# Spreading transfers over the steps of retention attention, and an earlier first product of the experts

## The chip, the cores and the metric

The kernel runs on one core of a Trainium2 chip. The metric is the time of one execution on the device in microseconds, as the median of several runs. The engines are named as in the profile: PE is TensorE (PEld its weight loads), DVE VectorE, ACT ScalarE, POOL GpSimd, and SP is SyncE, which here only issues transfers.

## The reference

The reference is retention attention followed by a mixture of experts.

```python
# q, k, v: 4 batches, 8 heads, 768 tokens, 64 wide
gamma = 1.0 - 2.0 ** (-5.0 - np.arange(H))
for t in range(S):
    state = gamma * state + k[t] (outer) v[t]          # per batch and head
    y[t] = q[t] @ state / sqrt(D)
x = y as 3072 tokens of 512
noisy = x @ w_gate + log1p(exp(x @ w_noise)) * noise    # 8 experts
top2 of noisy per token, weights by softmax over the two
out[token] += weight * (relu(x[token] @ w1[e]) @ w2[e])  # w1: 512x1024, w2: 1024x512
```

## The kernel before, in words

The 3072 tokens are 24 chunks of 128. One call of `step(j)` works on several chunks at once: PE multiplies q and k of chunk j+1 (`qk`, 8 matmuls into `pA`; the trace counts each fp32 matmul as two), turns the result of chunk j-1 (`x_turn`, into `pT`), adds the state's part of y for chunk j (`y_state`), adds the chunk's own part (`y_mm`, from the masked products `am` and the scaled values `vp`) and updates the state (`pU`, which ACT copies to U). DVE masks `pA` into `am`, works out the scale of a token row, and copies y out of PSUM as `yt`. ACT takes the sum of squares, the logits, `x` (L459) and its fp16 half. POOL makes `vp` (`v_scale`) and the low fp16 half of x (L465). SP issues the loads of chunk j+4 (`load`, 512 KB for q and k, 512 KB for v and k), and stores x into a buffer in memory (`x_store`). `AHEAD` is 4, so five tiles of each input are there. The order of the work on each engine is the order in which the program issues it; there is no planner. Work of other kinds is put at the end of a step by small tables: `at` and `P` with the number of the step (`todo`, `mid`), `at0` (`first_todo`, at the very end), and `middle` between `y_state` and `y_mm`.

Tokens' routing is worked out in three groups during and after the steps (`route_x` and what follows it). The experts' matmuls run in fp16 with each number split into a high and a low half. For the first expert this preparation lies in the steps: `w_load` brings a quarter of w1 (512 KB) into `wst`, `w_sum` takes squares on ACT, `w_scale` adds them on PE into the PSUM bank pR, DVE makes a power of two of it, `w_hi` rounds to fp16 on ACT, and `w_lo_half` makes half of a low part on DVE. The first expert's first 384 tokens are fetched from the buffer by three `gather` calls (an indirect DMA issued by POOL) and turned by three DMA transposes issued by SP (`x_t`), which write the tile `xe`. The first product of the experts (`first(0, ...)`, 12 matmuls of 384 columns, L918, L919 and L923) follows the last step; x_turn(23) stands in its middle. After it PE goes through all other products.

`HALVES` and `WHOLE` choose the form of `x_turn`: a chunk in `WHOLE` uses 4 matmuls of 128x144 (and a memset on DVE), the others 16 of 64x80.

## Time and profile before

| | |
|---|---|
| median of 3 runs | 643.45 us (642.65 to 644.96) |
| the profiled execution | 642.6 us, span 640.8 us, mean granted clock of TensorE 0.997 of full speed |
| PE busy | 627.5 us (98%) |
| ACT, DVE, POOL busy | 302.7, 290.4, 203.1 us |
| steps 0 to 23 | from the start to 110.40 us, where the second product begins |
| DMA | 113.03 MB, mean 176 GB/s |

The profiled execution took 1.8 us more than its span; the median of the three runs is 0.85 us above the profiled execution. Times in rows count from the span's start. A name in square brackets at a row's end is what the engine waited for; "issue" means that the profile shows nothing that it waited for.

### The profile page before, as it was taken

To read this page: it belongs to the slowest core of one execution; us is meant where nothing else is said; L and a number is where in the kernel's file an instruction comes from. 1 tells how busy PE (TensorE), PEld (TensorE's weight loads), DVE (VectorE), ACT (ScalarE), POOL (GpSimd) and SP (SyncE) were. 2 spreads that over 40 slices of the span, in tenths; PEclk is the share of its full clock that TensorE was granted. 3 is DMA by queue.
4 is the path that set the end of the run, shared out by engine and by line. 5 is a ranking of instruction groups with operands and counts; after the bars stand their busy time and mean duration, and the time that the engine had idled before them with its cause. 6 is when DMAs were issued, how large, how long until landed. Compare 5 with 4: busy or idle time off the path is not lost.

```text
span 640.8 us, 12702 instructions
## 1 busy us (share of the span) xinstructions
PE 627.5 (98%) x5151; PEld 380.8 (59%) x5151; DVE 290.4 (45%) x747; ACT 302.7 (47%) x582; POOL 203.1 (32%) x169
## 2 busy tenths in 40 slices
PE   9999989999999999999999999999999999999995
PEld 6888877559488545554455445544554465455574
DVE  4667887997453222653162236222622262215020
ACT  5688557516553443454344445434543454344121
POOL 2555575041530143114420432043304420430214
PEclk9999999999999999999999999999999999999998
DMA  8999995988868167727673667457744774572313
GB/s 304 407 408 405 351 370 135 368 198 294 177 133 262 25 110 137 266 44 133 115 222 108 104 129 209 133 94 127 209 142 87 135 202 141 97 125 44 42 18 43
DMA packets 87656, 113.03 MB, mean 176 GB/s; under 512 B 59910, under 2 KB 61068, under 8 KB 84012
## 3 DMA queue, kind: packets, MB, share of 16 engines
q1 hardware_dynamic: 75808, 85.56, 42.8%
q0 software_dynamic: 11776, 26.63, 22.5%
q8 instruction: 41, 0.67, 0.4%
q14 instruction: 19, 0.16, 0.1%
q10 hardware_dynamic: 12, 0.01, 0.0%
HBM read 72.66 MB, written 26.42 MB: 155 GB/s over the span
## 4 chain that ended last, share of the span: by engine, by line
PE 92%; DMA 3%; DVE 2%; ACT 1%; issue 1%; POOL 1%; SPq 0%; POOLq 0%; ACTq 0%
PE pH L918 13%; PE pH L919 13%; PE pH L921 13%; PE pO L967 12%; PE pO L969 12%; PE pO L968 12%; PE pA L368 3%; PE pY L392 3%; PE pT L1023 2%; PE pT L426 2%; DMA wst<-w 2%; PE pO L1011 2%; PE pY L385 2%; PE pT L416 1%; PE pU L402 1%; DMA in_vk<-vk 1%
## 5 line engine op out<-in xcount | busy, mean ns | idle before, releaser
L958 POOL DMA_INDIRECT out<-ot,idx x51 | 82.2, 1612 | 317.8 <-ACT ot L953 194.9
L918 PE MATMUL pH<-xe,w1h 128*128 128x384 f16 (+5 forms) x576 | 180.9, 314 | 0.1
L919 PE MATMUL pH<-xe,w1h 128*128 128x384 f16 (+5 forms) x576 | 180.8, 314 | 0.0
L921 PE MATMUL pH<-xe,w1l 128*128 128x384 f16 (+5 forms) x572 | 179.6, 314 | 0.0
L930 DVE SCALAR_TENSOR_TENSOR hl<-pH,hh 128x384 f16<-128x384 f32 (+5 forms) x144 | 75.6, 526 | 140.3 <-ACT hh L927 139.7
L969 PE MATMUL pO<-w2h,hl 128*128 128x512 f16 x344 | 130.4, 379 | 0.0
L968 PE MATMUL pO<-w2l,hh 128*128 128x512 f16 x344 | 130.4, 379 | 0.0
L967 PE MATMUL pO<-w2h,hh 128*128 128x512 f16 x344 | 130.4, 379 | 0.0
L927 ACT ACTIVATE hh<-pH 128x384 f16<-128x384 f32 (+5 forms) x144 | 67.1, 466 | 122.9 <-PE pH L921 112.1
L953 ACT ACTIVATE ot<-pO,gse 128x512 f32<-128x512 f32 x45 | 30.9, 687 | 155.1 <-PE pO L969 143.0
L240 DVE SCALAR_TENSOR_TENSOR w1l<-wst,wsc,w1h 128x1024 f16<-128x1024 f32 x28 | 35.9, 1284 | 95.4 <-ACT w1h L235 95.4
L918 PEld LDWEIGHTS <-w1h 128*128 128x128 f16 x576 | 56.3, 98 | 33.1 <-issue 2.7
L919 PEld LDWEIGHTS <-w1h 128*128 128x128 f16 x576 | 56.3, 98 | 30.1 <-issue 0.3
L921 PEld LDWEIGHTS <-w1l 128*128 128x128 f16 x572 | 55.9, 98 | 30.7
L771 POOL DMA_INDIRECT xg<-xbuf,idx x54 | 56.2, 1041 | 34.5 <-DVE idx L684 18.1
L212 ACT ACTIVATE junk<-wst 128x1024 bf16<-128x1024 f32 x64 | 67.0, 1047 | 0.3 <-DMA wst<-w 0.3
L969 PEld LDWEIGHTS <-hl 128*128 128x128 f16 x344 | 33.6, 98 | 40.6
L967 PEld LDWEIGHTS <-hh 128*128 128x128 f16 x344 | 33.6, 98 | 40.6 <-issue 0.4
L968 PEld LDWEIGHTS <-hh 128*128 128x128 f16 x344 | 33.6, 98 | 39.6
L465 POOL TENSOR_TENSOR x<-x,x 128x512 f16<-128x512 f32 x23 | 28.0, 1218 | 38.3 <-ACT x L464 17.8
L235 ACT ACTIVATE w2h<-wst,wsc 128x1024 f16<-128x1024 f32 x32 | 36.5, 1140 | 0.7 <-DVE wsc L190 0.7
L235 ACT ACTIVATE w1h<-wst,wsc 128x1024 f16<-128x1024 f32 x32 | 36.2, 1137 | 0.3 <-DVE wsc L190 0.3
(193 smaller groups left out, 661.8 us busy)
## 6 DMA issues: line engine op xcount, KB each, us to landing
wst<-w SPq DMA_DIRECT2D x28, 1024.0 KB, 7.6
in_qk<-qk SPq DMA_DIRECT2D x24, 512.0 KB, 8.2
in_vk<-vk SPq DMA_DIRECT2D x23, 512.0 KB, 8.3
xbuf<-x SPq DMA_DIRECT2D x24, 256.0 KB, 6.6
out<-zero SPq DMA_DIRECT2D x6, 1024.0 KB, 8.2
wst<-w SPq DMA_DIRECT2D x8, 512.0 KB, 7.3
xg<-xbuf,idx POOLq DMA_INDIRECT x54, 4.8
xe<-xg SPq DMA_TRANSPOSE x54, 4.7
```

Source lines behind the costliest of these rows:

```text
L212: nc.scalar.activation(junk, st[:, i * 1024:(i + 1) * 1024], AF.Square, accum_out=ss[:, i:i + 1])
L235: nc.scalar.activation(hi, st[:, i * 1024:(i + 1) * 1024], AF.Copy, scale=sc[:, 0:1])
L771: nc.gpsimd.indirect_dma_start(out=x[:n], out_offset=None, in_=xbuf[:128 + B0 * S] if e == 0 and t < 3 else xbuf, in_offset=bass.IndirectO ...
L918: nc.tensor.matmul(p[:, :n], whi, xh, start=(k == 0), stop=False)
L919: nc.tensor.matmul(p[:, :n], whi, xl, start=False, stop=False)
L921: nc.tensor.matmul(p[:, :n], wlo, xh, start=False, stop=(k == KT - 1))
L927: nc.scalar.activation(hh[:, f, n0:n1], p, AF.Relu)
L930: nc.vector.scalar_tensor_tensor(hl[:, f, n0:n1], p, 0.0, hh[:, f, n0:n1], op0=OP.max, op1=OP.subtract)
L958: nc.gpsimd.indirect_dma_start(out=out, out_offset=bass.IndirectOffsetOnAxis(ap=idx[:n, i:i + 1], axis=0), in_=ot[:n], in_offset=None, com ...
L967: nc.tensor.matmul(p, a, WT["2h"][:, f, :], start=(f == 0), stop=False)
L968: nc.tensor.matmul(p, a, WT["2l"][:, f, :], start=False, stop=False)
L969: nc.tensor.matmul(p, c, WT["2h"][:, f, :], start=False, stop=(f == FT - 1))
```

## The change

A step's transfers are issued in three parts. `load` of q and k (`qk`) is now issued at the step's start, the store of x after that, and the load of v and k (`vk`) after the store, with an added wait for the second `am` of the step (`SPREAD[0]`); of the inputs, three chunks are issued before the steps begin, no longer four. The loads of the first expert's weights get an added wait for the latest `yt` (`SPREAD[1]`). w1's quarters are loaded in steps 3, 6, 9 and 12, their sums taken in 6, 9, 12 and 14, and the scale and the high halves made in 15 to 18 (2 to 5, 5 to 8, and 9 to 12 before). The low halves that stood in steps 10, 11 and 12 are now in 17 to 20. w2's quarters are loaded in 15, 17, 18 and 19 (14 to 17 before). One gather stands at the end of step 17, and one each in steps 18 and 19 directly behind `v_scale`; before, two stood at the end of 17 and one at the end of 18. Chunk 22 leaves `WHOLE`. The first four matmuls of the first product come ahead of what is left of step 23, the other eight behind it, and x_turn(23) follows the product.

```diff
--- before.py
+++ after.py
@@ -61,7 +61,7 @@
 SOON = _C["vtab"][1]
 QW = HP * C + NC * HP
 WARM, BUSY = (5, 2), 3
-HALVES, WHOLE = [0, 2], [*range(4, 16, 2), 18, 20, 22]
+HALVES, WHOLE = [0, 2], [*range(4, 16, 2), 18, 20]
 XV = 128 + 2 * E
 
 
@@ -205,7 +205,9 @@
                             work.tile([128, 2], F32, name="wsc" + which, bufs=3))
         src = w1 if which == "1" else w2
         src = src[ds(order[e - 1], 1)].rearrange("a p c -> (a p) c") if e else src[0]
-        nc.sync.dma_start(ST[which, e][0][:, i * 1024:(i + n) * 1024], src[:, i * 1024:(i + n) * 1024])
+        p = nc.sync.dma_start(ST[which, e][0][:, i * 1024:(i + n) * 1024], src[:, i * 1024:(i + n) * 1024])
+        if not e:
+            behind(p, SPREAD[1], "weights at even distances")
 
     def w_sum(e, which, i):
         st, ss, sc = ST[which, e]
@@ -263,7 +265,11 @@
 
     AHEAD = 4
 
-    def load(j, pairs=("qk", "vk")):
+    def behind(p, q, reason):
+        tc.add_manual_dep(p.ins, q.ins.name, mybir.DependencyInfo(mybir.DependencyClass.Sync, mybir.DependencyReason.DATA),
+                          reason=reason)
+
+    def load(j, pairs=("qk", "vk"), after=None):
         for n in pairs:
             t = loads.tile([128, 2, DM], F32, name="in_" + n, bufs=AHEAD + 1)
             src = {"qk": qk_rows, "vk": vk_rows}[n][j]
@@ -271,7 +277,9 @@
                 for i in range(2):
                     nc.sync.dma_start(t[:, i], src[:, i * DM:(i + 1) * DM])
             else:
-                nc.sync.dma_start(t.rearrange("p a c -> p (a c)"), src)
+                p = nc.sync.dma_start(t.rearrange("p a c -> p (a c)"), src)
+                if after is not None:
+                    behind(p, after, "inputs at even distances")
             if n == "qk":
                 IN["q", j], IN["k", j] = [t[:, i].rearrange("p (a c) -> p a c", a=HP) for i in range(2)]
             else:
@@ -287,10 +295,11 @@
     nc.sync.dma_start(wgf, wgn)
     load(2, ("qk",))
     load(1, ("vk",))
-    for j in range(3, AHEAD):
-        load(j, ("qk",))
-        load(j - 1, ("vk",))
-    load(AHEAD - 1, ("vk",))
+    load(2, ("vk",))
+    due = {}
+    for j in range(3, NCH):
+        due.setdefault(j - AHEAD + (j <= 10), ([], []))[0].append(j)
+        due.setdefault(j - AHEAD + (j <= 14), ([], []))[1].append(j)
 
     nc.vector.tensor_scalar(mask, dif, 0.0, None, op0=OP.is_ge)
     nc.vector.tensor_scalar(ident, dif, 0.0, None, op0=OP.is_equal)
@@ -338,6 +347,7 @@
         u = loads.tile([128, HP, D], F32, name=f"U{i}", bufs=1)
         U.append(u)
 
+    SPREAD = {}
     VP, AM, PY, PT, YT, XS, X16, X32, LG = {}, {}, {}, {}, {}, {}, {}, {}, {}
     pctx = ExitStack()
     loop_psum = pctx.enter_context(tc.tile_pool(name="loop_psum", bufs=1, space=bass.MemoryType.PSUM))
@@ -370,7 +380,7 @@
         return pA
 
     def masked(j, pA, s):
-        nc.vector.tensor_tensor(AM[j][:, s], pA[s], mask[:, None, :].to_broadcast([128, HP, C]), op=OP.mult)
+        return nc.vector.tensor_tensor(AM[j][:, s], pA[s], mask[:, None, :].to_broadcast([128, HP, C]), op=OP.mult)
 
     def yplace(j, i, s):
         o = (i + s) % 2 * 64
@@ -393,7 +403,7 @@
                                  start=(not c and i < 2), stop=True, skip_group_check=True)
         YT[j] = loads.tile([128, 2, 2, C], F32, name="yt", bufs=1)
         y = YT[j].rearrange("p s g c -> p (s g c)")
-        nc.vector.tensor_tensor(y.rearrange("p (s x) -> p s x", s=2), PY.pop(j)[:, :, :2 * C],
+        SPREAD[1] = nc.vector.tensor_tensor(y.rearrange("p (s x) -> p s x", s=2), PY.pop(j)[:, :, :2 * C],
                                 gq[:, c].rearrange("p (s x) -> p s x", s=2), op=OP.mult)
         if c < NC - 1:
             for i in range(HP):
@@ -788,7 +798,7 @@
         o, n, i = block(e, t)
         nc.sync.dma_start_transpose(XE[e][:, :, o:o + n], XG[e, t][:n, :DM].bitcast(F16))
 
-    first_todo, middle, late = {}, {}, {}
+    first_todo, middle, late, early = {}, {}, {}, {}
 
     def at0(j, f, *a):
         first_todo.setdefault(j, []).append((f, a))
@@ -821,7 +831,7 @@
     P(17, slots, 0, 3)
     P(17, route_e, 0)
     for t in range(3):
-        at(17 + t // 2, gather, 0, t)
+        P(17 + t, gather, 0, t, d=early if t else todo)
         P(19 + t // 2, x_t, 0, t)
     at0(18, route_x, 1, 0, 6)
     P(19, route_b, 1, 0, 6)
@@ -840,14 +850,14 @@
     at(B0 * NC, turn_gate, 1)
     at(1, nc.vector.memset, zero, 0.0)
     for i in range(4):
-        at(2 + i, w_load, 0, "1", i)
-        at0(5 + i, w_sum, 0, "1", i)
-        at0(9 + i, w_hi, 0, "1", i)
-        at(14 + i, w_load, 0, "2", i)
+        at(3 + 3 * i, w_load, 0, "1", i)
+        at0((6, 9, 12, 14)[i], w_sum, 0, "1", i)
+        at0(15 + i, w_hi, 0, "1", i)
+        at((15, 17, 18, 19)[i], w_load, 0, "2", i)
         if i < 3:
-            at0((18, 20, 22)[i], w_sum, 0, "2", i)
-    first_todo[9].insert(0, (w_scale, (0, "1")))
-    for i, j in ((0, 10), (2, 11), (4, 12), (3, 21), (6, 22), (1, 22), (5, 23)):
+            at0((19, 21, 22)[i], w_sum, 0, "2", i)
+    first_todo[15].insert(0, (w_scale, (0, "1")))
+    for i, j in ((0, 17), (1, 18), (2, 19), (4, 20), (3, 21), (6, 22), (5, 23)):
         P(j, w_lo_half, 0, "1", i)
     at(3, nc.sync.dma_start, nz.rearrange("p c e -> p (c e)"), noise)
     at(3, nc.sync.dma_start, ct, ctab[:, SOON:])
@@ -869,6 +879,9 @@
         nc.tensor.matmul(t[:, 0], warm[:, :128], warm, start=True, stop=True)
     def step(j):
         more = j + 1 < NCH
+        now = due.get(j, ([], []))
+        for n in now[0]:
+            load(n, ("qk",))
         pA = qk(j + 1) if more else None
         if j:
             x_turn(j - 1)
@@ -877,17 +890,19 @@
             f(*a)
         if more:
             v_scale(j + 1)
+            for f, a in early.get(j, []):
+                f(*a)
             masked(j + 1, pA, 0)
-            masked(j + 1, pA, 1)
+            SPREAD[0] = masked(j + 1, pA, 1)
         if j:
             x_square(j - 1)
             x_scale(j - 1)
         if j < NC - 3:
             q_table(j + 3)
-        if j + AHEAD < NCH:
-            load(j + AHEAD)
         if j > 1:
             x_store(j - 2)
+        for n in now[1]:
+            load(n, ("vk",), SPREAD[0])
         if j:
             x_split(j - 1)
         if j == 0:
@@ -1044,8 +1059,8 @@
         return mm1_pe(0, 0, FIRST, f, between)
 
     j = NCH - 1
-    step(j)
-    p0 = first(0, lambda: x_turn(j))
+    p0 = first(0, lambda: step(j))
+    x_turn(j)
     lctx.close()
     hp = ctx.enter_context(tc.tile_pool(name="hp", bufs=1))
     XP.append(hp)
```

On PE, this is the scale of w1 before, at the end of step 9 (`pU`, then the scale, then the next `qk`):

```order
L402 MATMUL pU<-vp,in_vk 64x64 [waits DMAHW7_49]
L402 MATMUL pU<-vp,in_vk 64x64 x7
L222 LDWEIGHTS oneb
L222 MATMUL pR<-wsb_839,oneb 128x4 [waits Activation_49]
L368 MATMUL pA<-in_qk 128x128 [waits DMAHW5_49,DVE_49]
L368 MATMUL pA<-in_qk 128x128 [waits DVE_49]
```

and this after, where it stands at the end of step 15:

```order
L412 MATMUL pU<-vp,in_vk 64x64 [waits DMAHW4_49]
L412 MATMUL pU<-vp,in_vk 64x64 x7
L224 LDWEIGHTS oneb [waits DVE_49]
L224 MATMUL pR<-wsb_1281,oneb 128x4 [waits Activation_49]
L378 MATMUL pA<-in_qk 128x128 [waits DMAHW1_49,PE_49]
L378 MATMUL pA<-in_qk 128x128 [waits PE_49]
```

The pair of rows for `wsb` moved from one step's end to another's, and its weight load, which had no wait, now has one for DVE: pR holds the routing's sums until DVE has read them.

Also on PE, the last step before, from `pU` of step 22 on (`wide` is x_turn(22), L385 and L392 are step 23):

```order
L402 MATMUL pU<-vp,in_vk 64x64 x8
L416 MATMUL pT<-wide,yt 128x144 x4
L385 MATMUL pY<-in_qk,U_157 64x128 x8
L392 MATMUL pY<-am,vp 64x128 x8
L918 LDWEIGHTS w1h
L918 MATMUL pH<-xe,w1h 128x384
L919 LDWEIGHTS w1h
L919 MATMUL pH<-xe,w1h 128x384
L918 LDWEIGHTS w1h
L918 MATMUL pH<-xe,w1h 128x384
L919 LDWEIGHTS w1h
```

and the same place after:

```order
L412 MATMUL pU<-vp,in_vk 64x64 x8
L933 LDWEIGHTS w1h
L933 MATMUL pH<-xe,w1h 128x384
L934 LDWEIGHTS w1h
L934 MATMUL pH<-xe,w1h 128x384
L933 LDWEIGHTS w1h
L933 MATMUL pH<-xe,w1h 128x384
L934 LDWEIGHTS w1h
L934 MATMUL pH<-xe,w1h 128x384
L436 MATMUL pT<-turn,yt 64x80 x16
L395 MATMUL pY<-in_qk,U_153 64x128 x8
L402 MATMUL pY<-am,vp 64x128 x8
```

The four products moved ahead of x_turn(22) and all of step 23, and x_turn(22) became 16 narrow matmuls; behind these rows before stands x_turn(23), and after stand the other eight products and then x_turn(23).

On SP, the issues around the transposes of step 19 before (`in_qk`, `in_vk` are inputs, `xbuf` is the store of x, `xe` the transposes):

```order
L274 DMA in_qk<-qk 128x1024
L274 DMA in_vk<-vk 128x1024
L476 DMA xbuf<-x_1640 128x512
L789 DMA_TRANSPOSE xe<-xg 128x8x128 x2
L476 DMA xbuf<-x_1714 128x512
L789 DMA_TRANSPOSE xe<-xg 128x8x128
```

and after:

```order
L280 DMA in_qk<-qk 128x1024
L486 DMA xbuf<-x_1635 128x512
L280 DMA in_vk<-vk 128x1024
L799 DMA_TRANSPOSE xe<-xg 128x8x128 x2
L208 DMA wst_1381<-w 128x1024
L486 DMA xbuf<-x_1711 128x512
L799 DMA_TRANSPOSE xe<-xg 128x8x128
```

The load of v and k now follows the store, and a quarter of w2 (`wst_1381`) and a store stand between the second and the third transpose, where a store alone stood.

## Rows read from the trace of the kernel before

**Rows 1.** The page, part 1: busy us (share of the span) xinstructions of each engine.

```profile
PE 627.5 (98%) x5151; PEld 380.8 (59%) x5151; DVE 290.4 (45%) x747; ACT 302.7 (47%) x582; POOL 203.1 (32%) x169
```

**Rows 2.** Waits of PE, 0 to 110 us: waited for, us in total, times, longest.

```profile
PE pA L368 <- DVE am L373: 1.4, 1, 1.4
```

**Rows 3.** Timeline of PE, the four issue waits: start, us, operation, idle before.

```profile
37.51 0.44 PE L385 MATMUL pY<-in_qk,U 64*64 64x128 f32 x5 [0.62 <-issue]
...
43.68 0.39 PE L402 MATMUL pU<-vp,in_vk 128*64 128x64 f32 x6 [0.63 <-issue]
...
75.86 0.88 PE L392 MATMUL pY<-am,vp 128*64 128x128 f32 x12 [0.42 <-issue]
...
82.11 0.82 PE L368 MATMUL pA<-in_qk 64*128 64x128 f32 x10 [0.52 <-issue]
```

**Rows 4.** Timeline of PE, steps 22 to the second product.

```profile
104.02 1.22 PE L416 MATMUL pT<-wide,yt 128*128 128x144 f32 x8 [0.43 <-ACT U L404]
105.16 0.67 PE L385 MATMUL pY<-in_qk,U 64*64 64x128 f32 x16
105.76 1.09 PE L392 MATMUL pY<-am,vp 128*64 128x128 f32 x16
106.79 0.34 PE L918 MATMUL pH<-xe,w1h 128*128 128x384 f16 x1
...
108.38 0.78 PE L426 MATMUL pT<-turn,yt 64*64 64x80 f32 x32 [0.76 <-ACT x L459]
109.09 0.34 PE L918 MATMUL pH<-xe,w1h 128*128 128x384 f16 x1
...
110.40 0.33 PE L918 MATMUL pH<-xe,w1h 128*128 128x384 f16 x1
```

**Rows 5.** Windows of 10 us: us, busy by engine, PE clock, DMA share, GB/s.

```profile
30.00:40.00 10.00, 9.38 (x176) 8.19 (x174) 6.44 (x19) 8.14 (x20) 4.43 (x5) 1.00 1.03 405
90.00:100.00 10.00, 8.54 (x172) 7.41 (x170) 9.06 (x33) 5.39 (x14) 5.23 (x5) 1.00 1.26 325
```

**Rows 6.** DMA queues, 34 to 38 us: packets, MB, share of 16 engines.

```profile
q8 instruction: 1, 0.02, 1.6%
```

**Rows 7.** Timeline of DVE, 89 to 101 us.

```profile
89.69 3.45 DVE L502 TENSOR_TENSOR sp<-sp,nz 128x48 f32<-128x48 f32 x1
...
100.29 0.74 DVE L247 SCALAR_TENSOR_TENSOR w1l<-wst,wsc,w1h 128x512 f16<-128x512 f32 x1
```

**Rows 8.** Line L502, all four instructions: duration ns min/median/max, first and last start.

```profile
L502 DVE TENSOR_TENSOR sp<-sp,nz x4: 196/202/3446, 39.6 to 111.6; 128x48 f32<-128x48 f32 x4
```

**Rows 9.** Timeline of POOL, 88.9 to 93.1 us.

```profile
88.92 0.97 POOL L771 DMA_INDIRECT xg<-xbuf,idx  x1 [0.16 <-issue]
89.90 1.05 POOL L349 TENSOR_TENSOR vp<-in_vk,cs 128x512 f32<-128x512 f32 x1
90.90 1.17 POOL L465 TENSOR_TENSOR x<-x,x 128x512 f16<-128x512 f32 x1
92.02 1.04 POOL L349 TENSOR_TENSOR vp<-in_vk,cs 128x512 f32<-128x512 f32 x1
```

**Rows 10.** Timeline of PE, qk(21).

```profile
94.57 1.75 PE L368 MATMUL pA<-in_qk 64*128 64x128 f32 x16 [1.35 <-DVE am L373]
```

**Rows 11.** Timeline of all engines, end of step 15: qk(17) and the routing's posb.

```profile
72.76 1.16 PE L368 MATMUL pA<-in_qk 64*128 64x128 f32 x16
...
73.44 0.24 DVE L583 TENSOR_TENSOR posb<-pR,t 128x108 f32<-128x108 f32 x1
```

**Rows 12.** Timeline of ACT, the x of step 22.

```profile
107.64 0.69 ACT L459 ACTIVATE x<-pT,xsa 128x512 f32<-128x512 f32 x1 [1.26 <-DVE lgs L438]
```

**Rows 13.** Timeline of SP, the issues of the three transposes.

```profile
91.20 6.11 SPq L789 DMA_TRANSPOSE xe<-xg  x2
...
98.02 2.14 SPq L789 DMA_TRANSPOSE xe<-xg  x1
```

**Rows 14.** Tile xg, 80 to 105 us: landing of three gathers and three transposes.

```profile
DMA to landing us min/median/max: 4.1/6.9/7.3
```

## The prediction

> **What bounds the kernel now.** I read three views in this order: the waits of TensorE (PE) from the span's start to 110 us, the table of 10-us windows, and the timelines of the places that the waits name. PE is busy for 627.5 us, 98% of the span [rows 1], so the time is set by how soon PE gets through its list; what it wins before the second product of the experts, which starts at 110.40, can only be lost again to a wait that isn't there now. The waits before 110 us are few: 1.4 us for `am` of VectorE (DVE) [rows 2] and four pieces of 0.62, 0.63, 0.42 and 0.52, together 2.2 us, that the profile calls "issue" [rows 3]; two more stand in the last step [rows 4], 0.43 us for U and 0.76 for `x` of ScalarE (ACT). The windows [rows 5] say that the first piece lies where the 16 DMA engines are full (share 1.03 in 30 to 40 us), and that PE loses most, 1.46 of 10 us, in 90 to 100.
>
> The four issue waits look like late code. Queue q8, "instruction", moves one 16 KB packet in the stretch before and around the first of them [rows 6].
>
> The long wait for `am` starts on DVE [rows 7]. L502, a 128x48 multiply whose median over four is 0.20 us [rows 8], held DVE from 89.69 to about 93.1, 3.45 us; `am` (L373) stands behind it. In that time GpSimd (POOL) ran `vp`, `x`, `vp` back to back [rows 9], the third until 92.02 + 1.04 = 93.06, and then DVE is released. PE began qk(21) at 94.57 after 1.35 us of idleness for `am` and took 1.75 us for it [rows 10], against 1.16 us for the same matmuls in step 15 [rows 11]: 1.35 + 0.59 = 1.94 us lost.
>
> The Trainium skill has a rule for this (SBUF — State Buffer, "Who interferes with whom"): a DVE operation with two SBUF inputs and a GpSimd operation that reads SBUF exclude one another, and the one that comes first keeps the ports for one whole instruction. The trace agrees that DVE is shut out, but it was shut out through three POOL instructions, where one (1.17 us at most) would follow from the rule; by the rule alone the stretch has another cause and the 1.94 us would stay, which is the third rival's case.
>
> **The change part by part.** All times are on the scale of the profiled run (642.6 us, span 640.8); the median of three is 643.45, 0.85 us more, and I add that at the end.
>
> *Spacing of the loads.* The bytes are the same; w1 comes every third step, inputs are issued one at a time behind DVE's work. PE's list names no input that it waited for, so a later input costs nothing as long as it lands before its use; the loads still run three to four steps of about 4.3 us (24 of them before 105) ahead. What spacing can give back is the late code. A step asks for two inputs of 512 KB and stores 256 KB of x, about 1.3 MB in 4.3 us or 300 GB/s; four w1 parts of 512 KB within four steps bring that to 420, above the 405 GB/s of [rows 5], and the backlog lasts. One part every three steps makes 340, which the engines can do. The bounds are 0 and 2.2 us [rows 3]; I take two of the four waits, 1.2 us, those before 45 us, where this backlog is, and leave the two at 75 and 81 us, beside w2 loads that remain nearby.
>
> *Gathers one a step.* POOL's order in steps 18 and 19 was gather, vp, x, vp, x around L502; now each `vp` is followed by a gather and only then by `x`. A gather's own 0.97 us [rows 9] is then between the two POOL operations that shut DVE out, so L502 would slip in there. Bounds: 0 (it is held anyway) and 1.94 us; I take the whole, since the stretch needs three POOL operations without a gap. The extra half of w1l (L247, a DVE operation of 0.74 us [rows 7]) that now stands in step 19 behind L502 has room there once L502 is short; if L502 stays long it adds that to PE's wait, which puts the lower end at -0.74.
>
> *Scaling of w1 at step 15.* The w_scale matmul writes the PSUM bank pR, which at step 9 nobody used. At the end of step 15 it must wait until DVE has read the routing sums (L583, posb), and qk(17) stands behind it on PE. Before, qk(17) started at 72.76 and posb ended at 73.44 + 0.24 = 73.68 [rows 11]. So PE stops for about 0.95 us; ACT's and DVE's work behind qk(17) waits with it. The lower bound is 0.5 us if PE arrives a little later for other reasons, the upper 1.45 if the new chain of scales and w_hi (ACT) then also delays x_turn(16). The w_hi and w1l work that moves to steps 15 to 20 is hidden otherwise: ACT is busy 5.4 and DVE, without the 3.25 us of L502's hold, 5.8 of the 10 us from 90 to 100 [rows 5].
>
> So PE ends pU(22), 103.6 before (where the 0.43 us of idleness ahead of 104.02 begin [rows 4]), at 103.6 - 1.2 - 1.94 + 0.95 = 101.4.
>
> *The first product's place.* From 104.02 to 110.40 [rows 4] the old order has the wide turn (1.14), state (0.60), y (1.03), four products (4 x 0.165 = 0.66), a wait and its pipeline tail before the last turn (0.93), that turn (0.71) and eight products (1.31). The new order is four products 0.66, narrow turn 0.71, state 0.60, y 1.03, eight products 1.31, narrow turn 0.71: 5.0 us. The wait of 0.93 goes because between x_turn(22) and x_turn(23) there are now 2.94 us of PE work, of which ACT's x needs 0.69 [rows 12] and leaves 2.2 for the square and the scale before it; the wait of 0.43 for U goes as the products stand in between. With the narrower turn (0.43) that is 1.8 us.
>
> *What is late next.* The first product's weight load waits for all three transposes, and it stands ahead of step 23's state, y and turns, so a late transpose stops everything on PE. Before, the third was issued at 98.02 [rows 13] and took the shortest landing in the view, 4.1 us [rows 14]: 102.1, with 4.7 us to spare before 106.79. Now the product is due at 101.4. The transposes are issued by SP in order, two in 6.11 us and one in 2.14 [rows 13]; the third gather moves behind `vp` (89.90 + 1.05 - 88.92 = 2.0 us later at most [rows 9], with a landing of 6.9) and would land at 97.9, just when the third transpose could be issued anyway. Ahead of that transpose SP now also issues a 512 KB piece of w2 (I take 0.4 us, between nothing and the 0.7 us by which its other parts could hold SP), and a part of its bytes, 512 KB at 325 GB/s [rows 5] being 1.6 us, runs in front of the transpose. I take 0.4 + 0.6 us: landing at 103.1. PE waits 1.7 us there.
>
> The second product then starts at 103.1 + 5.0 = 108.1 instead of 110.40: 2.3 us sooner. Nothing behind it gets longer, and the whole rest moves. Forecast: 640.3 on the profiled scale, 643.45 - 2.3 = 641.15 as median.
>
> The Trainium skill (DMA: Bandwidth & Descriptors, "Queues, rings and completion order") speaks against the first part: each DMA engine takes turns between the queues that have work, a packet at a time, so a code packet would wait for a turn and not for the depth of the loads' queue. No row here shows the wait of a packet. By that rule thinner loads do not bring code sooner, and the 1.2 us would be 0, but the transposes, not PE's arrival, would still set the product unless the other terms fail too.
>
> **The rivals.**
> 1. *The transposes are no new wait.* With fewer bytes in flight in 80 to 100 us the gathers could land in 4 to 5 us rather than 6.9 (4.1 is the shortest landing in the same view [rows 14]), and the chain of transposes starts 2 us earlier: 101.1, before PE's 101.4. Then the product starts at 101.4, the second at 106.4: -4.0, 639.4. Against it: SP issues in order and the three transposes alone take 8.2 us of it; the loads of those steps remain.
> 2. *Slower: the third gather is a step late.* It now stands behind vp(20), which waits for in_vk(20); that load is issued behind DVE's `am`, where before it only followed its pair. If vp(20) comes one step later, at 94.2, the gather is issued at 95.2, lands 7.3 us later (the longest [rows 14]) at 102.5, the transpose at 106.6, with the w2 piece in front 108.2. The second product starts at 113.2: +2.8, 646.25. This decides from a landing of 105.4 on (105.4 + 5.0 = 110.4). For it: SP's waits in order, a full DMA (1.26 in 90 to 100 [rows 5]). Against it: the load still has over two steps.
> 3. *It does not do what it says.* The DMA is as full as before since the bytes are the same, the code stays late, L502 or another two-input operation is held, now with a half of w1l behind it; the new wait at step 15 is certain. PE arrives at 103.6 + 0.95 to 105.3, the product no longer waits for transposes, and the second starts at 109.6 to 110.3: -0.5 in the mean, 642.95.
>
> **How the numbers follow.** Forecast 0.43, rival 1 0.17, rival 2 0.13, rival 3 0.27. About 0.3%, 1.9 us, is what a measurement of this kernel can tell from no change, so "faster" begins at 641.5. The forecast's own range is 640.2 to 642.3, and about three fifths of it lie below 641.5: 0.26. With rival 1 that is 0.43. Slower is rival 2 and a little for holds that I do not see: 0.15. The rest, 0.42, is no change. The range runs from rival 1's 639.2 to 645.0, which takes in rival 3 and leaves out the far end of rival 2.
>
> **What would show it.** L502 (L512 now) at 0.2 us and no wait for `am` near 94 us; fewer "issue" waits before 50 us; a new wait of about 1 us ahead of qk(17) near 73 us, released by posb; the first product waiting 1 to 2 us for a transpose near 103; no wait ahead of x_turn(23). The prediction is wrong if the third transpose lands after 105.4 or before PE comes, if L512 is still over 1 us, or if loads are waited for by qk or pU in steps 11 to 22.

## The result and the profile after

The changed kernel takes 648.47 us (645.43 to 650.80), the kernel before beside it 644.32 us: ratio 1.0063, 95% interval 1.0039 to 1.0086, slower. A second measurement gave 1.0094 (1.0074 to 1.0115). The prediction was faster, 641.2 us with 645.0 as its upper end. The profiled execution is the shortest of its five, 645.43 us with a span of 643.6, against 642.6 and 640.8 before; so the profile shows a gap of 2.8 us where the medians show 4.

The page's busy times and three windows of 10 us, after, answer to [rows 1, 5]:

```profile
PE 626.3 (97%) x5175; PEld 380.1 (59%) x5175; DVE 286.7 (45%) x746; ACT 302.6 (47%) x582; POOL 203.5 (32%) x169
```

```profile
30.00:40.00 10.00, 9.07 (x174) 8.03 (x174) 6.39 (x17) 6.91 (x20) 4.67 (x5) 1.00 1.03 412
90.00:100.00 10.00, 8.75 (x176) 7.68 (x172) 8.35 (x39) 7.68 (x20) 7.07 (x7) 1.00 1.09 328
100.00:110.00 10.00, 6.33 (x162) 5.19 (x164) 5.04 (x18) 6.15 (x17) 4.66 (x6) 1.00 1.04 201
```

PE does the same work (626.3 us) in a longer span. The window from 90 to 100 us, where L502 was held before, gained 0.2 us, and that from 100 to 110 lost 2.5; before, it read:

```profile
100.00:110.00 10.00, 8.81 (x183) 6.96 (x180) 8.15 (x25) 7.27 (x18) 6.00 (x7) 1.00 0.34 101
```

The waits of PE from 0 to 112 us, after (what was waited for, us in total, times, longest), answer to [rows 2, 3]:

```profile
PE pH L933 <- DMA xe<-xg: 3.4, 1, 3.4
PE pT L436 <- ACT x L469: 1.6, 2, 1.3
PE pA L378 <- DMA in_qk<-qk: 0.9, 2, 0.7
PE pR L224 <- DVE posb L593: 0.9, 1, 0.9
...
PE pY L395 <- issue: 0.5, 1, 0.5
...
PE pR L552 <- issue: 0.3, 1, 0.3
```

The wait for `am` behind the held DVE operation is gone as predicted, the wait for posb is there as predicted, the issue waits are 0.8 instead of 2.2 us. New are inputs (0.9), `x` of ACT (1.6) and, largest, 3.4 us for the transposes. The rows left out here lie in the kernel's first 10 us; behind them PE is 0.2 us later than before (qk(2) starts at 11.46, before at 11.27). The timeline of PE around the first product, after, answers to [rows 4]:

```profile
103.70 0.64 PE L412 MATMUL pU<-vp,in_vk 128*64 128x64 f32 x16
107.72 0.32 PE L933 MATMUL pH<-xe,w1h 128*128 128x384 f16 x1 [3.39 <-DMA xe<-xg]
...
108.46 0.78 PE L436 MATMUL pT<-turn,yt 64*64 64x80 f32 x32
...
109.61 1.09 PE L402 MATMUL pY<-am,vp 128*64 128x128 f32 x16
110.64 0.34 PE L933 MATMUL pH<-xe,w1h 128*128 128x384 f16 x1
...
112.05 0.78 PE L436 MATMUL pT<-turn,yt 64*64 64x80 f32 x32
112.76 0.34 PE L933 MATMUL pH<-xe,w1h 128*128 128x384 f16 x1
```

The last `pU` ends at 104.34, 0.7 us later than before. PE then stands still until 107.72. From there to the second product at 112.76 it takes 5.04 us, the 5.0 of the sum. Before, the second product started at 110.40: 2.36 of the profile's 2.8 us lie here. The issues of SP, after, answer to [rows 13]:

```profile
92.69 6.83 SPq L799 DMA_TRANSPOSE xe<-xg  x2
99.61 0.53 SPq L208 DMA_DIRECT2D wst<-w  x1
100.24 1.16 SPq L486 DMA_DIRECT2D xbuf<-x  x1
101.49 1.31 SPq L799 DMA_TRANSPOSE xe<-xg  x1
```

The pair of transposes starts 1.5 us later than before and takes 6.83 us instead of 6.11, then a quarter of w2 and a longer store, and the third is issued at 101.49, 3.5 us later than before. The tile's transposes landed in (min, median, max):

```profile
DMA to landing us min/median/max: 6.1/7.7/9.2
```

The third lands 6.1 us after its issue, at 107.6, where the third of before took 4.1 [rows 14].

### The profile page after: what moved, and what is told of

It reads as the page before. It is cut to its first block, busy times and chain, and to the rows that moved or that the text cites. A ratio compares the mean times of both kernels' runs of the same rounds, so it can differ in the third digit from the quotient of the medians.

```text
span 643.6 us, 12756 instructions
## 1 busy us (share of the span) xinstructions
PE 626.3 (97%) x5175; PEld 380.1 (59%) x5175; DVE 286.7 (45%) x746; ACT 302.6 (47%) x582; POOL 203.5 (32%) x169
## 4 chain that ended last, share of the span: by engine, by line
PE 87%; DMA 5%; DVE 4%; SPq 2%; ACT 1%; issue 1%; POOL 0%; POOLq 0%; ACTq 0%; DVEq 0%
PE pH L933 13%; PE pH L934 13%; PE pH L936 13%; PE pO L982 12%; PE pO L984 12%; PE pO L983 12%; PE pY L402 2%; PE pA L378 2%; PE pT L1038 2%; PE pO L1026 2%; DMA in_qk<-qk 1%; DMA xg<-xbuf,idx 1%; PE pT L436 1%; PE pY L395 1%; SPq L799 1%; DMA xe<-xg 1%
```

## The experiments

Each kernel was compared with the kernel before on the same chip; the ratio and its 95% interval are given. Lines are those of the kernel that the edit starts from; "..." in a cut of code stands for lines left out.

### Undoing one part of the changed kernel

**The product's place undone** (the other parts stay):

```diff
-    p0 = first(0, lambda: step(j))
-    x_turn(j)
+    step(j)
+    p0 = first(0, lambda: x_turn(j))
```

> The changed kernel with one thing undone: the first product's first four matmuls stand again behind step 23's y, and x_turn(23) between them and the other eight. Theory (the place is what makes the late transposes costly: the second product starts at the landing of the third transpose + 5.0 us): step 23's narrow turn, state and y (0.71 + 0.60 + 1.03 us) run while the transposes are still under way, so the second product comes 2.3 us sooner, at about 110.4 instead of 112.76, and the time is 2.3 us below the changed kernel, about that of before + 0.4. Rival (PE's arrival, delayed by the w1 work in steps 15 to 19, sets the end): nothing is won, the time stays at the changed kernel's.

Measured: 1.0028 (1.0013 to 1.0043), against 1.0063: about 2.3 us won, as the theory says, and not back to before. In its profile the transposes are at least as late as in the changed kernel (the third issued at 102.62), but PE waits 0.7 us for them instead of 3.4, and the second product starts at 110.52.

**w2's steps undone**:

```diff
-        at((15, 17, 18, 19)[i], w_load, 0, "2", i)
+        at(14 + i, w_load, 0, "2", i)
-            at0((19, 21, 22)[i], w_sum, 0, "2", i)
+            at0((18, 20, 22)[i], w_sum, 0, "2", i)
```

> The changed kernel with w2's four loads again in steps 14 to 17 and its sums in 18, 20 and 22. Theory (SP issues a w2 piece of 512 KB ahead of the third transpose, and the piece's bytes run beside it): the third transpose is issued about 0.6 to 1.2 us sooner and lands in 4 to 5 us instead of 6.1, so landing moves from 107.6 to 105 or 105.9 and the time falls by 1.7 to 2.6 us. Rival (the chain of transposes is late from its first one on, because the first gather was issued 1.5 us later): only the 0.6 us of SP's issue are won.

Measured: 1.0037 (1.0018 to 1.0056), 1.7 us below 1.0063, the lower end of the theory's range. The two intervals overlap, so against that measurement alone the gain isn't shown; the second one of the changed kernel, 1.0094 (1.0074 to 1.0115), lies clear above. PE no longer waits for a transpose; but in this profile it came to the product at 106.0 itself, with 2.0 us of waiting for `x` at 95 us.

**The gathers undone**:

```diff
-        P(17 + t, gather, 0, t, d=early if t else todo)
+        at(17 + t // 2, gather, 0, t)
```

> The changed kernel with the gathers again two at the end of step 17 and one at the end of step 18. Theory (the first gather did not move, and the transposes go out in order behind its landing): the second and third gathers come 0.8 to 2 us sooner but the second and third transposes do not, the first product still waits; the time changes by less than 0.5 us. Rival (the gathers' new places make the transposes late): the third transpose lands 2 us sooner and the time falls by 2 us. DVE's L512 is at 0.2 us where POOL has a gather between vp and x, and may be held for 1 to 3 us again here.

Measured: 1.0063 (1.0042 to 1.0083), no change. The gathers' order is not the cause. PE waited 3.3 us for the transposes here too.

**w1's steps undone**:

```diff
-        at(3 + 3 * i, w_load, 0, "1", i)
+        at(2 + i, w_load, 0, "1", i)
-        at0((6, 9, 12, 14)[i], w_sum, 0, "1", i)
+        at0(5 + i, w_sum, 0, "1", i)
-        at0(15 + i, w_hi, 0, "1", i)
+        at0(9 + i, w_hi, 0, "1", i)
...
```

(with the scale again in step 9 and the low halves in 10, 11, 12, 21, 22, 22, 23)

> The changed kernel with w1's loads, sums, scale, high and low halves in the steps of before (2 to 5, 5 to 8, 9, 9 to 12, 10 to 12 and 21 to 23). Theory (w1's move delays the routing: 0.92 us of waiting for posb, 0.93 us for inputs at 31 and 35 us, so the first gather is issued 1.5 us later and the transposes with it): PE reaches the first product 2 us sooner, at about 102.3, the third transpose lands 1.5 us sooner, and the time falls by 1.5 us, not by more, since the product still waits. Rival (w1's move is what slows the kernel): the time falls by the whole 4 us to that of before or below it. The issue waits of 30 to 45 us return by 1.2 us if spacing w1 had removed them.

Measured: 1.0124 (1.0096 to 1.0151), above 1.0063 though not clear of the second 1.0094. Both the theory and its rival fail: with the new loads, w1 in steps 2 to 5 makes PE wait 2.4 us for inputs. So the loads of the inputs themselves became the suspect. The profile, the fastest of its six executions, also has a stop of 3.2 us at the first product with the clock at 0.50 behind it, and the other five executions have mean clocks of 0.989 to 0.994, so a part of this loss is likely the clock.

### One part alone, on the kernel before

**The product's place and the narrow turn** (and 22 out of `WHOLE`):

```diff
-    step(j)
-    p0 = first(0, lambda: x_turn(j))
+    p0 = first(0, lambda: step(j))
+    x_turn(j)
```

> The kernel before with two edits alone: the first product's first four matmuls ahead of step 23, x_turn(23) behind the product, and chunk 22 out of WHOLE. Theory (the place is sound where transposes land before PE comes): the third transpose lands at 102.1 and PE comes at 103.6 as before, so the second product starts at 108.6 instead of 110.4 and the time falls by 1.8 us (ratio 0.997). Rival (the place is what costs): PE waits for a transpose and the time rises by 2 us or more; if the wait is over 3 us the clock falls to half behind it, as it did in two runs above, and the loss grows by another 1.7 us.

Measured: 0.9992 (0.9980 to 1.0004), no change, and the theory's 0.997 is excluded. The profile has the second product at 108.79, 1.6 us sooner, and a new wait of 0.8 us behind it for `mb`, a tile that DVE makes for the last routing. Its span, 640.7 us, is only 0.1 below that of before, so about 1.5 us were given back; the list of waits accounts for 0.8 of it and for 0.3 more (`hl`, also of DVE).

**The loads in three parts with their waits**:

```diff
+        for n in now[0]:
+            load(n, ("qk",))
...
-        if j + AHEAD < NCH:
-            load(j + AHEAD)
+        for n in now[1]:
+            load(n, ("vk",), SPREAD[0])
```

(with the lead of the change, that is, the number of steps by which the issue of an input is ahead of its chunk's own step: three up to chunk 10 for q and k and up to chunk 14 for v and k, four behind them; and with the wait of w1's and w2's loads for yt)

> The kernel before with only the inputs' loads in three parts and the added waits for am and yt. Theory (later inputs cost PE time): waits of qk for in_qk of 1 to 2.4 us in all, as in the changed kernel (0.9) and its variants (1.6, 2.4), and an even later first gather; the time rises by 1 to 2 us. Rival (spacing frees the DMA engines): the four issue waits (2.2 us) shrink to under 1 us and the time falls by 1 us.

Measured: 1.0074 (1.0045 to 1.0103): as large a loss as the changed kernel's and more than the theory's 1 to 2 us. PE's waits there:

```profile
PE pA L378 <- DMA in_qk<-qk: 3.0, 2, 1.7
PE pY L402 <- issue: 1.8, 1, 1.8
```

Inputs are waited for: 1.70 us at 32.77, where w1 is loaded. The other 1.30 us lie at 7.89, at the kernel's start, and the kernel with the product's place and the narrow turn, whose loads are those of before, waited 1.40 us there too, so they don't belong to the new loads. The issue waits did not shrink (1.8, 0.9 and 0.7 us). The rival falls.

**w1's steps alone** (all its steps as in the change):

```diff
-        at(2 + i, w_load, 0, "1", i)
+        at(3 + 3 * i, w_load, 0, "1", i)
...
-    first_todo[9].insert(0, (w_scale, (0, "1")))
+    first_todo[15].insert(0, (w_scale, (0, "1")))
```

> The kernel before with only w1's work moved: loads in 3, 6, 9, 12, sums in 6, 9, 12, 14, scale at 15, high halves in 15 to 18, low halves in 17 to 23. Theory: 0.92 us of waiting for posb at qk(17) and 1 to 2 us of waiting for x of ACT in steps 16 to 19, behind the high halves and a held low half, against 1.2 us won from issue waits; the time rises by about 1 us. Rival (w1 thinned out is a gain, as the worse result with w1 put back suggests): waits for inputs and code vanish and the time falls by 1 us or more.

Measured: 1.0015 (1.0004 to 1.0025), 1 us slower, the theory. But the issue waits that the theory counted as won are there:

```profile
PE pU L402 <- issue: 1.1, 2, 0.6
PE pY L385 <- issue: 0.6, 1, 0.6
```

Two of the three, 0.62 us at 37.47 and 0.63 at 43.64, are the first two of before [rows 3]. Loading w1 in every third step does not remove them, and with the loads alone others came up at 66, 80 and 86 us. So neither of the two edits that were to thin out the transfers bears out the 1.2 us that I had put down for late code.

**The gathers one a step alone**:

```diff
-        at(17 + t // 2, gather, 0, t)
+        P(17 + t, gather, 0, t, d=early if t else todo)
...
+            for f, a in early.get(j, []):
+                f(*a)
```

> The kernel before with only the gathers moved, one a step and directly behind v_scale in steps 18 and 19. Theory: L502 runs in 0.2 us instead of 3.45, the wait of 1.4 us for am goes and the time falls by 1.9 us (ratio 0.997); the third transpose lands at 103 and is not waited for, since the first product still stands behind step 23's y. Rival: another two-input operation of DVE is held in its place, and nothing is won.

Measured: 0.9996 (0.9983 to 1.0010). The profile shows no wait for `am` and a span of 639.9, 0.9 below before; the comparison does not separate it from no change, and the theory's 1.9 us is excluded.

### What in the loads costs

**The changed kernel with a lead of four steps** (chunk 3 loaded ahead of the steps):

```diff
-        due.setdefault(j - AHEAD + (j <= 10), ([], []))[0].append(j)
-        due.setdefault(j - AHEAD + (j <= 14), ([], []))[1].append(j)
+        for a in range(2):
+            if j == AHEAD - 1:
+                load(j, (("qk", "vk")[a],))
+            else:
+                due.setdefault(j - AHEAD, ([], []))[a].append(j)
```

> The changed kernel with the inputs of all chunks issued four steps ahead, as before (chunk 3 ahead of the steps; q and k of chunk j at the start of step j-4, v and k in step j-4). Theory (a load of chunk j that is issued at the start of step j-3 has two steps, about 8.3 us, until qk(j) at the start of step j-1, and lands in 7.8): the 0.9 us of waiting for in_qk go, PE and with it the gathers and transposes come about 1 us sooner; the time is 1 to 2 us below the changed kernel, ratio about 1.003 to 1.005. Rival (the added waits for am and yt are the cost): no more than 0.3 us is won.

Measured: 1.0050 (1.0031 to 1.0070), which isn't clear of the changed kernel's 1.0063. No input is waited for in the steps any more (the list's only wait for in_qk, 1.4 us, is at 8.05, at the start). PE came to the product at 102.1, 2.2 us sooner than in the changed kernel, and waited nearly as long:

```profile
98.28 2.01 SPq L802 DMA_TRANSPOSE xe<-xg  x1
```

```profile
105.28 0.32 PE L936 MATMUL pH<-xe,w1h 128*128 128x384 f16 x1 [3.19 <-DMA xe<-xg]
```

The first row is SP's issue of the third transpose, at 98.28, as early as before (98.02 [rows 13]); the second is PE's first product. The transpose took 6.9 us to land with a w2 quarter ahead of it. An early issue alone does not bring it.

**Loads in three places, lead three, without the added waits**: the kernel above with the loads in three parts, less these lines:

```diff
-                if after is not None:
-                    behind(p, after, "inputs at even distances")
-        if not e:
-            behind(p, SPREAD[1], "weights at even distances")
```

> The kernel before with the loads in three places and the shorter lead of three steps, but without the added waits of loads for am and yt. Theory (the lead is the cost): as with the waits, 3 to 4.7 us slower than before (ratio 1.005 to 1.007), with 2 to 3 us of PE waiting for in_qk. Rival (the added waits are the cost): within 0.15% of before.

Measured: 1.0046 (1.0031 to 1.0062), just under the theory's range, with 3.4 us of waiting for in_qk, all of it between 32 and 43 us.

**The loads in three parts, with their waits and a lead of four** (the lead's edit stands above):

> The kernel before with the loads in three places and the added waits, but the lead of four steps. Theory (the lead is the cost): no wait for in_qk, within 0.15% of before. Rival (the added waits or SP's order are the cost): still 3 to 4.7 us slower.

Measured: 1.0021 (1.0009 to 1.0033). Between the two: no wait for in_qk is left, but 1.0 us for `vp` at 87.8, behind a later in_vk.

**The shorter lead alone, at the old place**:

```diff
...
-        if j + AHEAD < NCH:
-            load(j + AHEAD)
+        for a, b in zip(("qk", "vk"), due.get(j, ([], []))):
+            for n in b:
+                load(n, (a,))
```

(with `due` as in the change)

> The kernel before with nothing but the shorter lead: inputs up to chunk 10 (v and k up to 14) three steps ahead instead of four, at the old place of a step, without added waits. Theory (the lead is the cost): PE waits 2 us or more for in_qk between 20 and 40 us, where w1 is loaded, and the time rises by 3 to 4.7 us; since qk's load stands later in the step here, rather the upper end. Rival: within 0.15% of before.

Measured: 1.0018 (1.0005 to 1.0031): slower, but less than the theory said. The wait is where it was expected, and shorter:

```profile
32.23 1.16 PE L369 MATMUL pA<-in_qk 64*128 64x128 f32 x16 [1.14 <-DMA in_qk<-qk]
```

So the shorter lead costs something by itself (1.0018), the places and the added waits cost something without it (1.0021), and together they cost 1.0074. Whether the added waits cost anything by themselves isn't shown: the intervals with them (1.0074) and without (1.0046) overlap, and how the parts divide the loss isn't settled beyond that.

### The transpose and w2

**The last quarter of w2 in step 20 instead of 19**, on the changed kernel:

```diff
-        at((15, 17, 18, 19)[i], w_load, 0, "2", i)
+        at((15, 17, 18, 20)[i], w_load, 0, "2", i)
```

> The changed kernel with one load moved: the last quarter of w2 in step 20, behind the third transpose, instead of 19. Theory (that piece costs 0.6 us of SP and 2 us of landing): the third transpose is issued at 100.8 and lands at 105, PE waits under 1 us for it, the clock stays at full speed in nearly all runs, and the time falls by 2.5 us and by another 1 to 2 us in the runs whose clock fell: ratio 1.000 to 1.002 against 1.0063. Rival (the full DMA of those steps is the cost): less than 1 us is won.

Measured: 1.0030 (1.0015 to 1.0046), half of the loss gone with one load moved behind the third transpose: more than the rival's 1 us, but a smaller gain than the theory's 1.000 to 1.002. SP's issues, and PE's first product:

```profile
102.33 1.88 SPq L799 DMA_TRANSPOSE xe<-xg  x1
104.30 0.52 SPq L208 DMA_DIRECT2D wst<-w  x1
```

```profile
106.62 0.32 PE L933 MATMUL pH<-xe,w1h 128*128 128x384 f16 x1 [0.26 <-DMA xe<-xg]
```

The transpose is issued later than in the changed kernel (102.33; this execution lost 1.7 us to an input), yet lands in 4.2 us, and PE waits 0.26.

**Lead of four steps and w2's old steps**, on the changed kernel (both edits stand above):

> The changed kernel with the lead of four steps and w2's loads in steps 14 to 17 as before. Theory (w2 piece ahead of the third transpose, and the lead): PE reaches the first product at about 102, the third transpose is issued at 98.3 and lands in 4.3 us at 102.6, so PE waits under 1 us, the clock does not fall, and the second product starts at about 107.6; with 0.8 to 1.5 us given back behind it the time is 1 us below before (ratio 0.998 to 1.000). Rival (the transposes are late for another reason): a wait of 2 us or more stays, ratio 1.003 or more.

Measured: 0.9991 (0.9976 to 1.0007): the loss is gone. The transposes land in

```profile
DMA to landing us min/median/max: 4.1/6.7/7.4
```

and PE doesn't wait for them:

```profile
104.74 0.34 PE L936 MATMUL pH<-xe,w1h 128*128 128x384 f16 x1
```

The third, issued at 98.30, lands at 102.4. The two edits together account for the slowdown. By luck the ratio lies in the theory's range: PE came at 104.7 and not at 102, after 2.0 us of waiting for `x`, and the second product started at 109.79 instead of 107.6.

**w2's new steps alone**, on the kernel with place and gathers that stands below (ratio 0.9978 without them):

> The kernel with the product's place, the narrow turn and the gathers alone, and w2's loads and sums moved as in the change (15, 17, 18, 19). Theory (the w2 piece ahead of the third transpose is the cost): the third transpose is issued 0.6 us later and lands in 6 us or more instead of 4.3, at 105 or 106; PE, there at 103, waits 2 to 3 us, and the clock falls behind it in part of the runs; ratio 1.001 to 1.005, 2 to 4 us above the same kernel without w2's move. Rival (w2's move is harmless without the shorter lead): 0.998 as without it.

Measured: 1.0010 (0.9993 to 1.0027), 2 us above 0.9978 (0.9966 to 0.9990) without w2's move; the intervals just part. SP and PE:

```profile
97.62 0.57 SPq L208 DMA_DIRECT2D wst<-w  x1
...
99.54 1.30 SPq L789 DMA_TRANSPOSE xe<-xg  x1
```

```profile
105.47 0.32 PE L920 MATMUL pH<-xe,w1h 128*128 128x384 f16 x1 [3.14 <-DMA xe<-xg]
```

The quarter at 97.62 stands ahead of the third transpose, PE starts 5.9 us after that one's issue, and it has waited 3.14 us.

**The changed kernel a second time**:

> The changed kernel unaltered. Theory: the third transpose lands after 105.4 and PE stops for over 2 us; executions with a mean clock below 0.995 are the slower ones, by 2 us or more, and where the profile is one of them it shows the clock at 0.50 for about 3.5 us behind the stop. Ratio 1.005 to 1.008. Rival: the slow executions have no lower clock, and their time is lost in the steps.

Measured: 1.0094 (1.0074 to 1.0115), above the theory's range. Its profile shows what the first could not. PE's timeline and the windows of 1 us (busy by engine, the granted clock, DMA share, GB/s):

```profile
107.38 0.32 PE L933 MATMUL pH<-xe,w1h 128*128 128x384 f16 x1 [3.10 <-DMA xe<-xg]
...
108.85 1.10 PE L395 MATMUL pY<-in_qk,U 64*64 64x128 f32 x16
109.87 1.98 PE L402 MATMUL pY<-am,vp 128*64 128x128 f32 x16
```

```profile
107.00:108.00 1.00, 0.62 (x4) 0.32 (x4) 0.00 (x0) 0.00 (x0) 0.85 (x4) 1.00 0.95 361
108.00:109.00 1.00, 1.00 (x38) 0.88 (x40) 0.00 (x0) 0.00 (x0) 0.17 (x1) 0.79 0.00 0
109.00:110.00 1.00, 1.00 (x22) 0.67 (x16) 0.08 (x1) 0.80 (x3) 0.00 (x0) 0.50 0.81 182
110.00:111.00 1.00, 1.00 (x11) 1.00 (x13) 0.22 (x2) 0.65 (x1) 0.00 (x0) 0.50 0.35 129
111.00:112.00 1.00, 1.00 (x9) 0.58 (x8) 0.10 (x1) 0.97 (x3) 0.22 (x1) 0.50 0.00 0
112.00:113.00 1.00, 1.00 (x7) 0.59 (x6) 1.00 (x2) 0.95 (x3) 0.94 (x1) 1.00 0.00 0
```

After a stop of 3.1 us PE ran at full clock for about 1.2 us, then at 0.50, the 1.2 GHz level, until 112: y (L402) took 1.98 us instead of 1.09. The second product started at 113.99, 1.6 us later than 5.0 us behind the stop. In the first profile the stop was 3.4 us and the clock stayed at 1.00. The five executions of the first measurement, 645.43, 646.94, 648.47, 648.85 and 650.80 us, have mean clocks of 0.996, 0.994, 0.995, 0.992 and 0.990. As an estimate, 0.001 of mean clock over 645 us is about 0.65 us of PE, so the clock would account for 3.9 of the 5.4 us between the first and the last, but for only 0.6 of the 3.0 us of the third; where in these executions the clock was low, no trace shows. It doesn't order the second measurement either: its longest (650.88) has 0.996. A part of the spread has another cause, which stays open.

### Towards a faster version

**Place, narrow turn and gathers** (their edits stand above), with loads, w1 and w2 as before:

> The kernel before with the product's place, the narrow turn and the gathers one a step; loads, w1 and w2 as before. Theory: PE reaches the product at 102.6, the third transpose lands at 102.5 to 103.7, the second product starts at 107.7 to 108.7, 2 us sooner; 0.8 to 1.5 us are given back where the last routing is waited for (mb at the fourth product). Ratio 0.998 to 0.999. Rival (the place costs whatever stands around it): 1.000 or above.

Measured: 0.9978 (0.9966 to 0.9990), 642.55 against 643.83 us: faster than both kernels, with the interval below 1. PE's timeline:

```profile
103.22 0.32 PE L920 MATMUL pH<-xe,w1h 128*128 128x384 f16 x1
...
108.01 0.78 PE L426 MATMUL pT<-turn,yt 64*64 64x80 f32 x32 [0.40 <-ACT x L459]
108.73 0.34 PE L920 MATMUL pH<-xe,w1h 128*128 128x384 f16 x1
...
114.87 0.19 PE L540 MATMUL pR<-mb,trib 128*128 128x54 bf16 x1 [0.76 <-DVE mb L529]
```

The product does not wait, the second one starts 1.7 us sooner than before. x_turn(23) waits 0.40 us for `x`, and 0.76 us are given back at 114.87, where the last routing (`mb`) is late. The profile's span, 640.4 us, is 0.4 below that of before, so more than these 0.76 us of the 1.7 is lost again behind the product; the rest isn't traced.

**x_turn(23) ahead of the last four matmuls of the product**, on the same:

```diff
+        if then:
+            then()
         for k in range(KT if early else 0):
...
-    p0 = first(0, lambda: step(j))
-    x_turn(j)
+    p0 = first(0, lambda: step(j), lambda: x_turn(j))
```

> As c1, with x_turn(23) ahead of the first product's last four matmuls instead of behind them, so that the last routing starts 0.65 us sooner. Theory (the give-back is the last routing's wait for mb): it shrinks by 0.65 us and the time is 0.5 us below c1. Rival: the same as c1 within 0.1%.

Measured: 0.9983 (0.9970 to 0.9996), the same as without, as the rival says. The wait for `mb` fell from 0.8 to 0.4 us, and x_turn(23) waited 1.0 us for `x` instead of 0.4.

## Why the prediction was wrong

The step that failed is "What is late next", as I put it: "I take 0.4 + 0.6 us: landing at 103.1. PE waits 1.7 us there." The third transpose landed at 107.6. I had counted a w2 quarter as 1.0 us and taken the start and the length of the transposes as those of before. Where the quarter stands ahead of the third transpose, that one lands in 5.9 to 6.9 us (both profiles of the changed kernel, w2's steps alone, lead four; counted to PE's start where the trace has no landing) instead of 4.1 to 4.3 (before, w2 in its old steps with lead four, its last quarter in step 20, place and gathers), and the quarter's issue and the store behind it took 0.53 + 1.16 us of SP, where a store of 0.53 stood before. That is 2.0 us of landing and about 1.2 us of SP, 3.2 instead of 1.0. The other 2.2 us of the 5.5 by which the third transpose landed later than before came from the transposes' start, 1.5 us later, and from a pair that took 0.7 us longer. PE, due at 101.4, came at 104.34, still 3.3 us ahead of the landing, so the landing alone set the product's start.

The price that I had worked out for the second rival, a landing of 108.2, was nearly met, and by luck, since it came by another way: not by a late in_vk(20), since `vp` ran at 90.45 and the third gather went out at 91.65:

```profile
85.66 1.15 POOL L781 DMA_INDIRECT xg<-xbuf,idx  x1 [0.17 <-DVE am L383]
...
90.45 1.05 POOL L359 TENSOR_TENSOR vp<-in_vk,cs 128x512 f32<-128x512 f32 x1
91.65 0.98 POOL L781 DMA_INDIRECT xg<-xbuf,idx  x1 [0.16 <-issue]
```

- *Spacing of the loads.* "a later input costs nothing as long as it lands before its use": the condition failed. The load of chunk 7 was issued at 25.02 and used at 31.65:

```profile
25.02 0.38 SPq L280 DMA_DIRECT2D in_qk<-qk  x1
```

```profile
31.65 1.16 PE L378 MATMUL pA<-in_qk 64*128 64x128 f32 x16 [0.71 <-DMA in_qk<-qk]
```

  Before, it had been issued at 18.81. I had counted steps from the issue to the chunk's own step, but qk(j) runs at the start of step j-1, so a lead of three is two steps, about 8 us, less what SP is late by. In the profile that cost 0.9 us of PE; alone, the new loads cost 0.74%. The first gather went out 1.5 us later than before. The wait for posb by itself does not make it late: with a lead of four the changed kernel still waits 0.92 us for posb, and its first gather goes out at 83.75, against 84.14 before. Nor did the spacing empty the DMA engines where it was meant to: from 30 to 40 us their share is 1.03, as before. The 1.2 us for late code did appear in this profile (0.8 us of issue waits instead of 2.2), but with the loads alone there were 3.4, and with w1's steps alone the two waits before 45 us stayed, so spacing is not shown to be its cause. By the rule of the Trainium skill that I set beside this term (DMA: Bandwidth & Descriptors, "Queues, rings and completion order") it would be 0, as I wrote there. Those two kernels agree.
- *Gathers.* L512 ran in 0.20 us, as predicted, but the time came back:

```profile
86.42 2.03 DVE L249 SCALAR_TENSOR_TENSOR w1l<-wst,wsc,w1h 128x512 f16<-128x512 f32 x1
...
92.24 0.20 DVE L512 TENSOR_TENSOR sp<-sp,nz 128x48 f32<-128x48 f32 x1
```

```profile
92.83 0.78 PE L436 MATMUL pT<-turn,yt 64*64 64x80 f32 x32 [1.25 <-ACT x L469]
```

  The half of w1l that moved to step 18 was held in its place (2.03 instead of 0.74 us), while POOL ran `vp` from 86.84 to 87.89; the reduction behind it, ACT's work on it and the high half of w1 queued up, and x_turn waited 1.25 us for `x`. I had named such a hold only as a part of the third rival, and PE's arrival at 104.3 is near that rival's (104.55), not the forecast's 101.4. From 11 us to pU(22) the lists of waits come to -1.4 us for issue, +0.9 for inputs, +0.9 for posb, +1.6 for `x` and -1.6 for `am` and the slow qk behind it. With the 0.2 us of the start that is 0.6 of the 0.75 us by which pU(22) ended later, where I had forecast 2.2 sooner.
- *Scaling of w1.* 0.92 us for posb, 0.95 predicted. Right, though w1's steps alone make a loss (1.0015).
- *The first product's place.* 5.04 us, 5.0 predicted. Right; but the sentence "Nothing behind it gets longer" was wrong. With x_turn(23) after the product the last routing is waited for by 0.3 to 0.8 us, and the place that wins 1.6 us up to the second product in its own profile is worth nothing that can be measured by itself (0.9992).
- *Not in the sum at all:* the clock behind the stop. It cost 1.6 us in the second profile. That it also makes the medians differ by more than the first profile shows is likely, by the mean clocks above, but no trace shows it.
- *The range.* Rival 1 comes to 639.4 us, and the range begins at 639.2; rival 2's 646.25 lies outside it altogether, not by its far end. Neither slip changes the account.

The Trainium skill (TensorE: Matmul & The Clock Gate, "Part 1: The HAM clock gate") says that the array is clocked at half rate when it has lately been idle, and warns of idle gaps inside a kernel. The second profile agrees, with a granted clock of 0.50 after the stop of 3.1 us; the first, with 1.00 after 3.4 us, shows that the length of the stop alone does not decide.

## What to carry to other kernels

When work is moved ahead of a wait, the transfer that it waits for has to be followed from its first issue, with what stands ahead of it in the issuing queue: here it landed 5.5 us later than before, where the move was to save 1.8 us. A lead in steps is to be counted from the issue to the instruction that reads the tile, in us, against the landing time in the profile. And parts that each look neutral should be timed alone: here the product's place and the gathers paid together (0.9978), and the loads, w1 and w2 made a loss of it.

## What the runs showed of the hardware that was not expected

- The third DMA transpose, of 128 tokens, landed 4.1 to 4.3 us after its issue, and 5.9 to 6.9 us with a 512 KB load issued ahead of it. The first two of each kernel, issued as a pair, took 6.2 to 9.2 us where the traces show it.
- After PE stops of 3.1 to 3.3 us the clock fell to 0.50 for 3 to 4 us in four of the profiles (gathers undone, w1's steps undone, w2's new steps alone, the second of the changed kernel), and not in two others with stops of 3.2 (lead four) and 3.4 us (the first of the changed kernel).
- Issue waits up to the second product ranged from none (the changed kernel with lead four) to 3.4 us (the loads alone) among kernels whose transfers were alike in bytes, with the DMA engines full from 30 to 40 us in both kernels (share 1.04 and 1.03); nothing here settles what sets them.
